# An output projection in seven half-size products instead of eight, on pairs of 128-row blocks

## The chip, the cores and the metric

The kernel runs on one core of a Trainium2 chip. The metric is the device time of one execution in microseconds, here the median of three runs. Five engines work side by side: TensorE (PE in the profile, with its weight loads as PEld), VectorE (DVE), ScalarE (ACT), GpSimd (POOL) and SyncE (SP), which issues nearly all the DMAs here. TensorE writes its sums to PSUM, in banks of 512 columns of f32; VectorE and ScalarE read them from there, GpSimd works on SBUF alone.

## The reference

One token sequence x of 2048 rows and 512 columns goes two ways, and a gate per row mixes the results:

```
a   = x @ dft_hid_re.T ;  b = x @ dft_hid_im.T
A   = dft_seq_re @ a - dft_seq_im @ b                 # 2048 x 2048 by 2048 x 512, twice
q, k, v = split(x @ wqkv), 32 heads of 16
o   = softmax(q k^T / 4, causal, window 256) @ v
B   = o @ wo                                          # 2048 x 512 by 512 x 512
g   = sigmoid(sum(x * gate_w))
out = g * A + (1 - g) * B
```

All is f32. To keep the precision, every f32 operand of a matrix product is split in two parts, hi and lo, and three products are summed: hi hi, hi lo and lo hi (`TERMS`).

## The kernel before

The rows are handled in 16 blocks of 128 (`tb`). Attention runs as a pipeline over four head groups and 32 key blocks; the dense work (projections, then the DFT along the sequence) is a Python generator, `dense`, from which a few TensorE instructions at a time are put between those of attention. TensorE's order is therefore written out by hand. For VectorE, ScalarE, GpSimd and SP a planner sets the order after the first instructions, by its own estimate of when each instruction can start; `behind` and `late` only hold an instruction back until a named earlier one has been issued.

A DFT block (`c_block`, and `c_final` for block 15) takes 16 chunks of 3 matmuls of 512 columns (L528). Its weights come from raw pieces of `cr` and `ci`, 512 KB each, that are loaded ahead into two `raw` buffers and split by VectorE (`split_soon`; the profile shows these under L587, the line of `late`) into three `hi`/`lo` buffers. Finished blocks are scaled by the gate and stored to scratch in DRAM (`r_scr`), and `add_r` lists their numbers in `wait`. The attention output lies in DRAM as well (`o_scr`, transposed, four groups g of 128 rows).

When attention has ended, `attention_done` reuses its large buffers: `fin` in the place of `ring0` holds the split `wo`, `os` in the place of `ring1` holds split attention blocks. From then on `c_part` calls `tail_step` after every fourth chunk, so every twelve DFT matmuls. These calls are the steps, counted from 0 by `clock`. The output projection is done there:

- `wo_prep(tb)` loads one attention block (256 KB, in runs of 512 bytes) and splits it: ScalarE makes hi, VectorE lo (L80, L85). Up to seven blocks are kept ahead.
- `wo_block` runs, three steps later at the earliest and two blocks to a step, 4 groups x 3 terms = 12 matmuls of 512 columns (L811) into one PSUM bank, loads the stored DFT row `r` and adds the two with the gate on VectorE (L813); `tail_step` stores the sum to `out`.

For blocks 14 and 15 the projection comes before the end of the DFT; the sum is kept in `mixed`, and `add_r` and `c_final` add the DFT part to it. `wo` is loaded in `attention_done` into the two `raw` buffers. The steps that begin the two last DFT pieces are in `c_final`: four chunks each at steps 9, 10 and 11, two at step 12, and at the end the last two chunks in halves of 256 columns (L558), each followed by a VectorE instruction (L560) and a store (L561).

PSUM has four banks for `st` (the `ps_a` pool: attention scores, then the projection), two for attention outputs and two for the dense work.

Of the kernel before, what the change touches and what calls it, by code (L numbers as in the profile page):

```python
# [7 lines left out]
F32 = mybir.dt.float32  # L8
F32R = mybir.dt.float32r
AF = mybir.ActivationFunctionType  # L10
OP = mybir.AluOpType
# [3 lines left out]
P = 128  # L15
# [3 lines left out]
NG = 4  # L19
NP = 4  # L20
BQ = 64
NB = S // BQ
WIN = 320
# [4 lines left out]
SWITCH = 6  # L28
# [4 lines left out]
def fnet_window_mix(ctx: ExitStack, tc: tile.TileContext, xT, x, wqk, wv, wr, wi, cr, ci, wo, gw, out):  # L33
    nc = tc.nc

    const = ctx.enter_context(tc.tile_pool(name="const", bufs=1))
    big = ctx.enter_context(tc.tile_pool(name="big", bufs=16))
    st = ctx.enter_context(tc.tile_pool(name="st", bufs=3))
    ev = ctx.enter_context(tc.tile_pool(name="ev", bufs=5))
    at = ctx.enter_context(tc.tile_pool(name="at", bufs=2))  # L40
    ps_a = ctx.enter_context(tc.tile_pool(name="ps_a", bufs=4, space=PSUM))
# [36 lines left out]
    def split(hi, lo, raw, act=False):  # L78
        if act:
            nc.scalar.copy(hi, raw)  # L80
# [4 lines left out]
        return nc.vector.tensor_sub(lo, raw, f(hi))  # L85
# [57 lines left out]
    def pt_raw():  # L143
        return at.tile([P, NP, WIN], F32, name="pt", bufs=4).rearrange("p a b -> p (a b)")[:, :1024]
# [290 lines left out]
    def t_pair(n, p):  # L435
        q0 = n % NB * BQ
        w = min(WIN, S - q0)
        if p == 0:
            if "proj" in have:
                more.append(n)  # L440
            c = (n - more[0]) % 6 * NP * WIN if more else 3072
            if c + NP * WIN <= 3072:
                PT[n] = f(home[:, c:c + NP * WIN].rearrange("p (a b) -> p a b", a=NP))
            else:
                PT[n] = at.tile([P, NP, WIN], F32, name="pt", bufs=4)
        pt = PT[n]
        ps = ps_a.tile([P, 512], F32, name="t", tag="st")
        nc.tensor.matmul(ps[:, :w], PAD[1, n][:, p], ring[0][:, p, q0:q0 + w], start=True, stop=True)  # L448
        nc.scalar.activation(pt[:, p, :w], ps[:, :w], AF.Exp, scale=-1.0)  # L449
        if p % 2:  # L450
            ph = slice(p - 1, p + 1)
            a = pt[:, ph, 0:64]
            nc.gpsimd.affine_select(a, a, pattern=[[0, 2], [2, 64]], compare_op=OP.is_ge, fill=0.0,  # L453
                                    base=1, channel_multiplier=-1)
# [88 lines left out]
    def c_final(get, ab):  # L543
        ps = ps_d.tile([P, 512], F32, name="dc", tag="d")
        g = g1[:, 15:16]
        for j in range(2):
            w = get((1, 30 + j))
            yield from c_part(w, range(16)[8 * j:8 * j + 8 - 2 * j], ab, ps, (0, 13))
            yield
        while wait:  # L550
            tail_step()
        r = mixed.pop(15)
        late(nc.vector.scalar_tensor_tensor, r, ps, g, r, OP.mult, OP.add)
        for c, dma in ((slice(0, 256), nc.sync), (slice(256, 512), nc.scalar)):
            ps2 = ps_a.tile([P, 512], F32, name="t", tag="st")
            for i in (14, 15):
                for a, b in TERMS:
                    nc.tensor.matmul(ps2[:, c], w[a][:, i % 8 * 128:i % 8 * 128 + 128], ab[SC[i]][:, b, c],  # L558
                                     start=i == 14 and a + b == 0, stop=i == 15 and a == 1)
            nc.vector.scalar_tensor_tensor(r[:, c], ps2[:, c], g, r[:, c], op0=OP.mult, op1=OP.add)  # L560
            dma.dma_start(out[15][:, c], r[:, c])  # L561
        yield
# [197 lines left out]
    now = []  # L760
    wait = []
    mixed = {}
    born = {}
    clock = iter(range(99))

    def tail_step():
        t = next(clock)
        for tb in [tb for tb in O if born[tb] < t - 2][:2]:
            if tb in wait:
                wait.remove(tb)  # L770
                ld(out[tb], wo_block(tb, 1))
            else:
                mixed[tb] = wo_block(tb, 0)
        for tb in (*wait[:5], 15, 14, *wait[5:]):
            if tb not in O and tb not in mixed and len(O) < 7 and (tb > now[-1] or tb in wait):
                wo_prep(tb)
                born[tb] = t

    def attention_done():
        fin = const.tile([P, 8192], F32R, name="fin", tag="ring0")  # L780
        ORAW.extend(f(fin[:, 4112 + 512 * i:4624 + 512 * i]).rearrange("p (g t) -> p g t", g=NG) for i in range(7))
        fin = fin[:, 16:4112].rearrange("p (j c h e) -> p j c h e", j=2, c=2, h=2)
        OS.append(const.tile([P, 8, 2, NG, P], F32R, name="os", tag="ring1"))
        for j in range(2):
            raw = st.tile([P, 1024], F32, name="raw", bufs=2)
            ld(raw, wo[j])
            for c in range(2):
                split(fin[:, j, c, 0], fin[:, j, c, 1], raw[:, c * 512:c * 512 + 512])
        FIN.append(fin)

    OS = []
    ORAW = []
    O = {}
    slot = iter(range(99))

    def wo_prep(tb):
        oraw = ORAW[0]
        ORAW.append(ORAW.pop(0))
        ld(oraw, o_scr[tb // 4][:, :, tb % 4 * P:tb % 4 * P + P].rearrange("g p t -> p g t"))
        O[tb] = OS[0][:, next(slot) % 8]  # L800
        split(O[tb][:, 0], O[tb][:, 1], oraw[:], True)

    def wo_block(tb, half):
        o = O.pop(tb)
        r = ev.tile([P, 512], F32, name="ev")
        ld(r, r_scr[half if half or tb < 16 - SWITCH else 2][tb])
        ps = ps_a.tile([P, 512], F32, name="t", tag="st")
        n = 0
        for g in range(NG):
            for a, b in TERMS:  # L810
                nc.tensor.matmul(ps, o[:, a, g], FIN[0][:, g // 2, g % 2, b], start=n == 0, stop=n == 11)  # L811
                n += 1
        nc.vector.scalar_tensor_tensor(r, ps, g0[:, tb:tb + 1], r, op0=OP.mult, op1=OP.add)  # L813
        return r


    stream = dense()
# [46 lines left out]
    for n in range(N + LAG + 1):  # L864
        k = n - LAG
        if k == 0:
            masks.append(n)
        ring_ahead(n + 1)
        if k in (-1, 4):
            v_spread(0 if k < 0 else 4)  # L870
        if k in (-4, -1, 4):
            v_next({-4: 0, -1: 4, 4: 8}[k])
        if n == 0:
            make_pad(0, 0)
        for p in range(NP):
            if n < N:
                s_pair(n, p)
            fill(n)
            visit = p == 0 and (k - summed >= (6 if more else 4) or k == N)
            if 0 <= k < N and not visit:  # L880
                t_pair(k, p)
            if p == 0:
                make_pad(0, n + 1)
                if k >= -1:
                    make_pad(1, k + 1)
            fill(n)
            if visit:
                for j in range(summed, k):
                    pv(j)
                summed = k  # L890
                if k < N:
                    t_pair(k, p)
            for at_n, at_p, do in TURN if n > 12 else FIRST:
                u, j = divmod(n - at_n, 8)
                if p == at_p and j == 0 and 0 <= u < 16:
                    do(u)
            if p == 3 and k % 8 == 6 and 0 <= k < N:
                l_load(k // 8)
            if p == 0 and full:
# [55 lines left out]
```

## Time and profile before

| | |
|---|---|
| median of 3 runs | 850.38 us (850.13 to 850.64) |
| the profiled execution | 850.96 us, its span 849.0 us |
| granted TensorE clock | 1.000 |
| projection matmuls, L811 | 192, 45.5 us busy, mean 392 ns |
| DFT matmuls, L528 | 1530, 344.5 us (hi) and 200.3 us (lo) busy |
| ScalarE cast of an attention block, L80 | 16, mean 621 ns |
| VectorE subtraction of an attention block, L85 | 16, mean 682 ns |
| VectorE gate and sum of a projected block, L813 | 16, mean 748 ns |
| `fin<-o_scr`, `ev<-r_scr` and `out<-ev` loads and stores | 256 KB each |

The busy time of a matmul overlaps that of the next, since they are pipelined: the time from one start to the next is shorter than the mean. Line numbers are those of the kernel before; a helper's line (L56 for loads and stores, L80, L82 and L85 for splits, L587 for what goes through `late`) stands for all its callers, so the names of the tiles tell which work it is. In a line of the timeline the first number is the start, the second the time from the first start to the last end, and x the number of instructions in it.

### The profile page before, as it was taken

Reading aid. Unit: us, or ns where it says so; the run is one execution under the profiler, and the core shown is the slowest. Engines: PE = TensorE matmul, PEld = TensorE weight load, DVE = VectorE, ACT = ScalarE, POOL = GpSimd, SP = SyncE. Lnnn points to the kernel's source line nnn. Section 1 sums busy time; section 2 is a strip of 40 time slices with the busy share of each in tenths; the row PEclk is TensorE's granted clock in tenths of the full one; section 3 lists DMA queues with packets and bytes.
Section 4 is the critical chain, followed back from the end, with each engine's and each line's share of the span. In section 5 each row is a group of like instructions: output and inputs, shape, how many; then the busy total and the mean of one; then the engine's idle time right before and its main releaser. Section 6 shows DMA issues by size and latency. Waiting matters only on the chain.

```text
span 849.0 us, 16711 instructions
## 1 busy us (share of the span) xinstructions
PE 843.7 (99%) x5166; PEld 691.4 (81%) x5166; DVE 611.3 (72%) x1999; ACT 593.6 (70%) x1798; POOL 256.8 (30%) x578
## 2 busy tenths in 40 slices
PE   9999999999999999999999999999999999999998
PEld 6888888888888788888888887888887878878887
DVE  5588978667978787787787886887987864437531
ACT  6488888878888897787877886877777865532100
POOL 8102332233332233342323333343233364620000
PEclk9999999999999999999999999999999999999999
DMA  8776678476765275533454557969774435339732
GB/s 296 244 228 186 214 243 257 181 233 225 216 222 178 63 211 134 171 115 123 137 158 127 177 150 227 308 216 306 254 215 134 138 121 164 128 118 333 225 134 75
DMA packets 94345, 160.99 MB, mean 190 GB/s; under 512 B 26800, under 2 KB 35760, under 8 KB 94256
## 3 DMA queue, kind: packets, MB, share of 16 engines
q1 hardware_dynamic: 93824, 159.28, 60.2%
q8 instruction: 40, 0.66, 0.3%
q10 hardware_dynamic: 432, 0.66, 0.2%
q14 instruction: 49, 0.40, 0.1%
HBM read 108.27 MB, written 51.64 MB: 188 GB/s over the span
## 4 chain that ended last, share of the span: by engine, by line
PE 94%; DMA 2%; DVE 2%; issue 1%; SPq 0%; ACT 0%; DVEq 0%; ACTq 0%
PE dc L528 39%; PE dqk L280 9%; PE dab L303 9%; PE t L448 9%; PE s L366 8%; PE o L474 8%; PE t L811 5%; PE dv L303 5%; DMA raw<-wo 1%; DMA ev<-l_scr 1%; PE s L268 1%; DVE sm L368 1%; PE dv L592 0%; SPq L56 0%; DVE pad L349 0%
## 5 line engine op out<-in xcount | busy, mean ns | idle before, releaser
L528 PE MATMUL dc<-big,hi 128*128 128x512 f32 x1020 | 344.5, 393 | 0.0
L371 ACT ACTIVATE sm<-sm,ml 128x320 f32<-128x320 f32 (+4 forms) x512 | 277.4, 543 | 59.6 <-DVE ml L368 54.1
L368 DVE CUSTOM_DVE_ANT_0 sm<-s,mask 128x320 f32<-128x320 f32 (+4 forms) x512 | 235.0, 464 | 108.6 <-PE s L366 73.2
L449 ACT ACTIVATE pt<-t 128x320 f32<-128x320 f32 (+4 forms) x392 | 159.8, 411 | 87.7 <-PE t L448 82.1
L528 PE MATMUL dc<-big,lo 128*128 128x512 f32 x510 | 200.3, 393 | 0.0
L528 PEld LDWEIGHTS dc<-big,hi 128*128 128x128 f32 x1020 | 180.4, 188 | 22.6
L448 PE MATMUL t<-ring,pad 128*128 128x320 f32 (+4 forms) x512 | 156.8, 306 | 0.1
L453 POOL TENSOR_SCALAR_AFFINE_SELECT pt<-pt 128x128 f32<-128x128 f32 x196 | 71.2, 363 | 283.3 <-ACT pt L449 279.7
L366 PE MATMUL s<-ring,pad 128*128 128x320 f32 (+4 forms) x512 | 155.3, 303 | 0.3 <-DVE ml L368 0.2
L349 DVE TENSOR_SCALAR pad<-ring,half 96x256 fp32r<-96x256 f32 x384 | 120.4, 360 | 11.9 <-PE t L448 11.7
L448 PEld LDWEIGHTS t<-ring,pad 128*128 128x128 f32 x512 | 96.1, 188 | 31.1 <-issue 8.7
L366 PEld LDWEIGHTS s<-ring,pad 128*128 128x128 f32 x512 | 96.2, 188 | 21.7 <-DVE ml L368 2.0
L528 PEld LDWEIGHTS dc<-big,lo 128*128 128x128 f32 x510 | 95.9, 188 | 11.9
L371 ACT ACTIVATION_READ_ACCUMULATOR sm<-sm,ml 128x1 f32 x512 | 97.4, 190 | 0.0
L587 DVE TENSOR_TENSOR lo<-raw,hi 128x512 fp32r<-128x512 f32 x137 | 93.8, 694 | 0.1
L303 PE MATMUL dab<-hi,big 128*128 128x512 f32 x256 | 89.0, 394 | 0.0
L280 PE MATMUL dqk<-big,hi 128*128 128x512 f32 x240 | 85.0, 393 | 0.0
L431 POOL TENSOR_SCALAR vpad<-vr,half 128x256 f32<-128x256 f32 x64 | 61.3, 969 | 65.3 <-PE o L474 30.3
L587 DVE CAST hi<-raw 128x512 fp32r<-128x512 f32 x137 | 57.7, 431 | 20.5 <-PE dc L528 17.0
L347 ACT ACTIVATE pad<-ring,half 96x256 fp32r<-96x256 f32 x128 | 66.8, 522 | 0.0
L457 POOL TENSOR_SCALAR_AFFINE_SELECT pt<-pt 128x128 f32<-128x128 f32 x172 | 60.8, 354 | 0.0
L474 PE MATMUL o<-pt,vpad 128*32 128x320 f32 (+4 forms) x1072 | 57.7, 351 | 0.0
(96 smaller groups left out, 912.5 us busy)
## 6 DMA issues: line engine op xcount, KB each, us to landing
qk_scr<-home SPq DMA_DIRECT2D x32, 512.0 KB
ring<-qk_scr SPq DMA_DIRECT2D x32, 512.0 KB
raw<-cr SPq DMA_DIRECT2D x32, 512.0 KB
raw<-ci SPq DMA_DIRECT2D x32, 512.0 KB
r_scr<-ev SPq DMA_DIRECT2D x42, 256.0 KB
ev<-r_scr SPq DMA_DIRECT2D x42, 256.0 KB
ab_scr<-home SPq DMA_DIRECT2D x20, 512.0 KB
big<-ab_scr SPq DMA_DIRECT2D x20, 512.0 KB
```

Source lines behind the costliest of these rows:

```text
L280: nc.tensor.matmul(ps, w[a][:, c:c + 128], XT[dk, ss][:, b], start=n == 0, stop=n == 11)
L303: nc.tensor.matmul(ps, XT[dk, ss][:, a, c * 128:(c + 1) * 128], wh[b], start=n == 0, stop=n == 11)
L349: nc.vector.tensor_scalar(dst, src, half[:96, h:h + 1], None, op0=OP.mult)
L366: nc.tensor.matmul(ps[:, :w], PAD[0, n][:, p], ring[1][:, p, k0:k0 + w], start=True, stop=True)
L368: mark("dve", nc.vector.tensor_tensor_reduce(out=sm[:, :w], in0=ps[:, :w], in1=mask[:, WIN - w:], scale=1.0, scalar=3e38, op0=OP.add, op1= ...
L371: mark("act", nc.scalar.activation(sm[:, :w], sm[:, :w], AF.Exp, bias=nm[:, c], scale=-1.0, accum_out=l[:, c]))
L448: nc.tensor.matmul(ps[:, :w], PAD[1, n][:, p], ring[0][:, p, q0:q0 + w], start=True, stop=True)
L449: nc.scalar.activation(pt[:, p, :w], ps[:, :w], AF.Exp, scale=-1.0)
L453: nc.gpsimd.affine_select(a, a, pattern=[[0, 2], [2, 64]], compare_op=OP.is_ge, fill=0.0, base=1, channel_multiplier=-1)
L474: nc.tensor.matmul(OT[g, sb][32 * p:32 * p + 32, q - sb * 512:e - sb * 512], v2[:, p], pt[:, p, q - q0:e - q0], start=first, stop=kb == 8 ...
L528: nc.tensor.matmul(ps, w[a][:, i % 8 * 128:i % 8 * 128 + 128], ab[SC[i]][:, b], start=i == ends[0] and a + b == 0, stop=i == ends[1] and a ...
L587: return fn(*args)
```

## The change

The output projection takes the blocks in eight pairs and computes each pair as a 2 x 2 block product: rows (two blocks a and b) by halves of the depth, times halves of the depth by halves of the columns of `wo`. The Strassen-Winograd scheme does this with seven products of half depth and half width (two depth chunks x three terms = 6 matmuls of 256 columns each) in place of eight, with sums of the inputs ahead of it and of the products behind it.

- `wo_fetch` loads `wo` with the last step of the attention loop, into two buffers of the pool of the probability tiles (`pt`), not into `raw`.
- `attention_done` forms four differences of quarters of `wo` (t1 to t4, GpSimd, 512 wide) and splits seven operands in place of four (three casts of them on ScalarE). Six buffers of attention (`vpad`, `pad`) take the raw attention blocks, three pairs of them; t1 to t4 are in four of the same. `rt`, in the place of `home`, holds the r rows of three pairs.
- `wo_load` loads the two attention blocks of a pair, at steps 0, 1 and 4 to 9.
- `wo_split`, two steps later or more (steps 4 to 11), loads the two r rows, makes the four sums s1 to s4 of 128 x 256 on GpSimd, and splits 512, 256 and 1024 columns (ScalarE hi, VectorE lo) into one of two slots of `os`.
- `wo_begin`, at the next step (5 to 12): four products p1, p6, p7, p5, each in a PSUM bank; ScalarE copies p1, VectorE adds p6 to it, and five VectorE operations (`into`) put p7, p5 and that sum (three times) into the rows.
- `wo_end`, at the step after (6 to 13): the closing three products go on top of p1, p7 and p5, and three `into` finish the rows, which are stored or kept in `mixed`.

So within a step TensorE does the three closing products of one pair, the four first ones of the next, and twelve DFT matmuls. `c_final` runs steps until nothing is open, and step 13 (the closing products of the last pair) lies ahead of the last halves.

```diff
-        while wait:
+        while wait or O:
             tail_step()
...
     def tail_step():
         t = next(clock)
-        for tb in [tb for tb in O if born[tb] < t - 2][:2]:
...
+        for stage, at_t in ((wo_end, 6), (wo_split, 4), (wo_begin, 5)):
+            if 0 <= t - at_t < 8:
+                stage(t - at_t)
+        if t < 2 or 4 <= t < 10:
+            wo_load(t if t < 2 else t - 2)
+
+    def wo_fetch():
+        for j in range(2):
+            WO.append(pt_raw())
+            ld(WO[j], wo[j])
 
     def attention_done():
         fin = const.tile([P, 8192], F32R, name="fin", tag="ring0")
...
-        for j in range(2):
-            raw = st.tile([P, 1024], F32, name="raw", bufs=2)
-            ld(raw, wo[j])
-            for c in range(2):
-                split(fin[:, j, c, 0], fin[:, j, c, 1], raw[:, c * 512:c * 512 + 512])
+        fin = fin[:, 16:7184].rearrange("p (m h c e) -> p m h c e", m=7, h=2, c=2)
+        OS.append(const.tile([P, 2, 4096], F32R, name="os", tag="ring1"))
+        RT.append(const.tile([P, 6, 512], F32, name="rt", tag="home"))
+        b11, b12, b21, b22 = (w.rearrange("p (c n e) -> p n c e", c=2, n=2)[:, n] for w in WO for n in range(2))
+        t1, t2, t3, t4 = (const.tile([P, 2, 256], F32, name="tw", tag=f"pad{i}_{j}")[:] for i in range(2)
+                          for j in range(2))
+        for t, x, y in ((t1, b12, b11), (t3, b22, b12), (t2, b22, t1), (t4, b21, t2)):
+            nc.gpsimd.tensor_sub(t, x, y)
+        for m, t in enumerate((b11, b21, b22, t4, t1, t2, t3)):
+            split(fin[:, m, 0], fin[:, m, 1], t, m % 2)
+        for tag in ("vpad0", "vpad1", "pad0_0", "pad0_1", "pad1_0", "pad1_1"):
+            ORAW.append(const.tile([P, NG, P], F32, name="oraw", tag=tag))
         FIN.append(fin)
...
+    def wo_load(i):
+        pair = [15, 14] if i == 2 else [wait.pop(0) for _ in range(2)]
+        raw = []
+        for tb in pair:
+            raw.append(ORAW.pop(0))
+            ORAW.append(raw[-1])
+            ld(raw[-1], o_scr[tb // 4][:, :, tb % 4 * P:tb % 4 * P + P].rearrange("g p t -> p g t"))
+        O[i] = pair, [t[:].rearrange("p g t -> p (g t)") for t in raw]
+
+    def wo_split(i):
+        pair, (a, b) = O[i]
+        k = 4 if i == 2 else i % 2 * 2
+        r = RT[0][:, k], RT[0][:, k + 1]
+        for tb, t in zip(pair, r):
+            with behind("sp"):
+                ld(t, r_scr[2 if i == 2 else 1][tb])
+        extra = at.tile([P, NP, WIN], F32, name="pt", bufs=4).rearrange("p a b -> p (a b)")
+        s1, s2, s3, s4 = (extra[:, 256 * k:256 * k + 256] for k in range(4))
+        nc.gpsimd.tensor_add(s1, b[:, :256], b[:, 256:])
+        nc.gpsimd.tensor_sub(s3, a[:, :256], b[:, :256])
+        nc.gpsimd.tensor_sub(s2, s1, a[:, :256])
+        nc.gpsimd.tensor_sub(s4, a[:, 256:], s2)
+        o = OS[0][:, i % 2, 16:3600].rearrange("p (h m) -> p h m", h=2)
+        for c, src in ((slice(0, 512), a), (slice(512, 768), b[:, 256:]), (slice(768, 1792), extra[:, :1024])):
+            split(o[:, 0, c], o[:, 1, c], src, True)
+        O[i] = pair, r, extra, o.rearrange("p h (m c t) -> p h m c t", m=7, c=2)
+
+    def wo_begin(i):
+        pair, (r1, r2), extra, o = O[i]
...
+        p1, p6, p7, p5 = (ps_a.tile([P, 512], F32, name="t", tag="st")[:, lo] for _ in range(4))
+
+        def product(ps, m, n, start=True):
+            for c in range(2):
+                for a, b in TERMS:
+                    nc.tensor.matmul(ps, o[:, a, m, c], FIN[0][:, n, b, c], start=start and c == 0 and a + b == 0,
+                                     stop=c == 1 and a == 1, skip_group_check=True)
+
+        def into(r, t, g):
+            nc.vector.scalar_tensor_tensor(r, t, g, r, op0=OP.mult, op1=OP.add)
+
+        u, u2 = extra[:, 1024:1280], extra[:, :256]
+        product(p1, 0, 0)
+        nc.scalar.copy(u, p1)
+        product(p6, 4, 5)
+        nc.vector.tensor_add(u2, p6, u)
+        product(p7, 5, 6)
+        into(r2[:, hi], p7, gb)
+        product(p5, 3, 4)
+        into(r2[:, hi], p5, gb)
+        into(r1[:, hi], u2, ga)
+        for c in (lo, hi):
+            into(r2[:, c], u2, gb)
+
+        def rest():
+            product(p1, 1, 1, False)
+            into(r1[:, lo], p1, ga)
+            product(p7, 2, 3, False)
+            into(r2[:, lo], p7, gb)
+            product(p5, 6, 2, False)
+            into(r1[:, hi], p5, ga)
...
+            if k == N - 1 and p == 3:
+                wo_fetch()
```

More of the change, by code (lines that the diff above doesn't have):

```diff
@@ L762, in fnet_window_mix @@
     mixed = {}
-    born = {}
     clock = iter(range(99))
@@ L767, in tail_step @@
         t = next(clock)
-        for tb in [tb for tb in O if born[tb] < t - 2][:2]:
[L769 to L777, printed above, removed]
+        for stage, at_t in ((wo_end, 6), (wo_split, 4), (wo_begin, 5)):
+            if 0 <= t - at_t < 8:
+                stage(t - at_t)
@@ L779, in attention_done @@
+        if t < 2 or 4 <= t < 10:
+            wo_load(t if t < 2 else t - 2)
+    WO = []
+    def wo_fetch():
+        for j in range(2):
+            WO.append(pt_raw())
+            ld(WO[j], wo[j])
     def attention_done():
         fin = const.tile([P, 8192], F32R, name="fin", tag="ring0")
-        ORAW.extend(f(fin[:, 4112 + 512 * i:4624 + 512 * i]).rearrange("p (g t) -> p g t", g=NG) for i in range(7))
-        fin = fin[:, 16:4112].rearrange("p (j c h e) -> p j c h e", j=2, c=2, h=2)
-        OS.append(const.tile([P, 8, 2, NG, P], F32R, name="os", tag="ring1"))
@@ L789, in attention_done @@
         FIN.append(fin)
     OS = []
+    RT = []
     ORAW = []
     O = {}
[L794 to L814, printed above, removed]
+    def wo_load(i):
[6 more added lines that the diff above has]
+        O[i] = pair, [t[:].rearrange("p g t -> p (g t)") for t in raw]
@@ new lines, in wo_begin @@
+    def wo_begin(i):
+        pair, (r1, r2), extra, o = O[i]
+        ga, gb = (g0[:, tb:tb + 1] for tb in pair)
+        lo, hi = slice(0, 256), slice(256, 512)
+        p1, p6, p7, p5 = (ps_a.tile([P, 512], F32, name="t", tag="st")[:, lo] for _ in range(4))
[25 more added lines that the diff above has]
+            into(r1[:, hi], p5, ga)
+            for tb, r in zip(pair, (r1, r2)):
+                if i == 2:
+                    mixed[tb] = r
+                else:
+                    ld(out[tb], r)
+        O[i] = rest
@@ L817, in fnet_window_mix, with wo_end @@
+    def wo_end(i):
+        O.pop(i)()
     stream = dense()
```

## The prediction

> **What bounds the kernel now.** I read the page's engine shares and slices first, to see who is busy at the end.
>
> ```profile
> span 849.0 us, 16711 instructions
> PE 843.7 (99%) x5166; PEld 691.4 (81%) x5166; DVE 611.3 (72%) x1999; ACT 593.6 (70%) x1798; POOL 256.8 (30%) x578
> ...
> PE   9999999999999999999999999999999999999998
> ...
> DVE  5588978667978787787787886887987864437531
> ...
> POOL 8102332233332233342323333343233364620000
> ```
>
> TensorE is busy to the last slice; VectorE and GpSimd thin out in the last four, which hold the output projection. The chain of work that ended last shows whether TensorE sets the end there.
>
> ```profile
> 759.31 6.52 DMA raw<-wo
> ...
> 768.52 5.94 DMA raw<-wo
> ...
> 775.90 4.17 PE t L811 x17
> 780.08 2.74 PE dc L528 x12
> 782.82 5.50 PE t L811 x24
> 788.31 2.72 PE dc L528 x12
> ...
> 832.10 5.50 PE t L811 x24
> 837.59 6.80 PE dc L528 x30
> 844.39 1.44 PE t L558 x12
> 845.83 0.02 issue
> 845.86 0.48 DVE ev L560
> ```
>
> From 775.90 on the chain is one unbroken run of matmuls. A step takes 5.50 us for two output blocks and 2.72 us for twelve DFT matmuls, eight times; then come the last DFT chunks and one VectorE instruction. The windows of two early steps and a late one show the cover.
>
> ```profile
> 765.80:774.00 8.20, 8.20 (x37) 6.78 (x37) 7.51 (x14) 3.10 (x5) 0.00 (x0) 1.00 1.06 322
> 774.00:782.20 8.20, 8.08 (x35) 6.31 (x34) 6.60 (x13) 2.81 (x5) 0.00 (x0) 1.00 1.14 331
> 798.70:806.90 8.20, 8.20 (x38) 6.75 (x37) 2.70 (x4) 1.24 (x2) 0.00 (x0) 1.00 0.34 115
> ```
>
> The columns are TensorE, weight loads, VectorE, ScalarE, GpSimd, then clock, DMA share, GB/s. VectorE is nearly full (7.51 of 8.20) and the DMA engines are full just where the projection starts; later both have room. GpSimd does nothing. So shorter matmul work here is paid out one for one, if the early part doesn't break.
>
> **1. The matmuls.** Per pair of blocks, 2 x 12 matmuls of 512 columns (L811) become 7 products x 2 chunks x 3 terms = 42 of 256 columns. The old spacing, then the only 256-column stream of this kind, at the end:
>
> ```profile
> 774.01 6.06 PE L811 MATMUL t<-fin,os 128*128 128x512 f32 x24
> ...
> 782.65 5.66 PE L811 MATMUL t<-fin,os 128*128 128x512 f32 x24
> ```
>
> ```profile
> 844.46 0.28 PE L558 MATMUL t<-big,lo 128*128 128x256 f32 x1
> ...
> 845.54 0.28 PE L558 MATMUL t<-big,lo 128*128 128x256 f32 x1
> ```
>
> The old pair takes 5.50 us (chain), 229 ns each. The two L558 rows are the third and the twelfth of a run in which every matmul loads its own weights: 1.08 us over nine intervals, 120 ns. So 42 x 0.120 = 5.04 us, 0.46 less per pair, and 8 x 0.46 = **3.7 us less**. The Trainium skill ("TensorE: Matmul & The Clock Gate", Back-to-back issue gap) has N/2.4 + 2.5 ns, so 216 and 109 ns, and by that estimate the saving would be 0.6 us a pair, 4.8 in all. The rows here are 11 to 13 ns above it at either width, and an overhead per matmul hurts the 42 more than the 24.
>
> **2. The start.** The first old run lasts 6.06 us against 5.66: it waited 0.40 us for the split weights. That wait goes; what is late next is the new preparation. The first new pair starts two steps later in the step count than the old (step 5, not 3), so at 774.01 + 2 x 2.73 = 779.5, and its second product, which needs the sums, 0.72 later: 780.2.
>
> wo now lands in the buffers of the last probability tiles, which these matmuls release:
>
> ```profile
> 761.59 0.54 PE L474 MATMUL o<-pt,vpad 128*32 128x128 f32 x16
> ```
>
> So its load leaves at about 761.9 on SP's queue, where the old one left at 759.31; loads queued behind it wait too, the raw DFT pieces among them. With the old 6.5 us it lands at 768.4, and at 765 if the DMA engines are freer (fewer attention blocks are fetched ahead). Then GpSimd makes four 512-wide differences, and for the first pair four 256-wide sums. Its rows, and VectorE's beside them:
>
> ```profile
> L587 POOL TENSOR_TENSOR lo<-raw,hi x5: 1295/1302/1430, 68.0 to 88.2; 128x512 fp32r<-128x512 f32 x5
> ```
>
> ```profile
> 67.95 1.66 DVE L349 TENSOR_SCALAR pad<-ring,half 96x256 fp32r<-96x256 f32 x2
> ```
>
> ```profile
> 68.03 2.72 POOL L587 TENSOR_TENSOR lo<-raw,hi 128x512 fp32r<-128x512 f32 x2
> ```
>
> ```profile
> L349 DVE TENSOR_SCALAR pad<-ring,half x384: 334/345/1392, 31.8 to 750.9; 96x256 fp32r<-96x256 f32 x192
> ```
>
> ```profile
> 757.63 0.78 POOL L453 TENSOR_SCALAR_AFFINE_SELECT pt<-pt 128x128 f32<-128x128 f32 x1 [1.25 <-ACT pt L449]
> ...
> 760.76 0.29 POOL L453 TENSOR_SCALAR_AFFINE_SELECT pt<-pt 128x128 f32<-128x128 f32 x1 [1.25 <-ACT pt L449]
> ```
>
> ```profile
> 757.58 1.37 DVE L587 TENSOR_TENSOR lo<-raw,hi 128x512 fp32r<-128x512 f32 x2
> ...
> 769.62 3.09 DVE L85 TENSOR_TENSOR os<-fin,os 128x512 fp32r<-128x512 f32 x5
> ```
>
> A 512-wide GpSimd two-input operation takes 1.30 us. No row has a 256-wide one: it lies between half (0.65) and the whole (1.30); I take 0.7, near the half, as the work follows the width. Together 4 x 1.30 + 4 x 0.7 = 8.0 us. Then the two engines block each other: a GpSimd select takes 0.78 us beside VectorE's two-input subtraction and 0.29 alone, and L349's median of 0.345 grows to as much as 1.39: its two at 67.95 run into GpSimd's subtractions of 68.03. A GpSimd operation may wait for one VectorE subtraction (0.6 to 0.68): 0 to 8 x 0.68 = 5.4 us in all. After it come ScalarE's cast and VectorE's subtraction of the 1024-wide sums:
>
> ```profile
> 10.81 1.14 ACT L80 CAST hi<-raw 128x512 fp32r<-128x512 f32 x2 [0.34 <-DMA raw<-wv]
> ```
>
> 1.14 us by two 512 casts, and 1.28 for two subtractions (0.60 + 0.68). GpSimd must thus be done by 780.2 - 2.4 = 777.8. Earliest: 765 + 8.0 = 773, early by 5 us. Latest: 768.4 + 8.0 + 5.4 = 781.8, late by 4.0. The middle (766.7 + 8.0 + 2.7 = 777.4) just holds. I book 0.7 us, from 0 to 4.0, and -0.40 for the old wait. Seven weight splits in place of four add three subtractions and no VectorE cast (three of seven casts are ScalarE's): 1.8 us more in a stretch where VectorE has little room; that is within the 4.0.
>
> **3. The steady steps.** A step is 5.04 + 2.72 = 7.76 us of matmuls. VectorE's rows:
>
> ```profile
> 7.97 0.42 DVE L163 TENSOR_TENSOR lo<-pt,hi 128x256 fp32r<-128x256 f32 x1
> 8.30 0.68 DVE L85 TENSOR_TENSOR big<-pt,big 128x512 fp32r<-128x512 f32 x1
> ```
>
> ```profile
> 844.43 0.75 DVE L587 SCALAR_TENSOR_TENSOR ev<-dc,g,ev 128x512 f32<-128x512 f32 x1 [6.05 <-PE dc L528]
> 845.28 1.06 DVE L560 SCALAR_TENSOR_TENSOR ev<-t,g,ev 128x256 f32<-128x256 f32 x2
> ```
>
> Subtractions follow each other every 0.33 us at 256 columns, 0.60 at 512 (3.09 for five), about 1.14 at 1024: 2.07. Six operations that read PSUM (the sum u2 and five `into`), 256 wide, between 0.33 and 0.48: 0.40, so 2.4. Three `into` from u2 in SBUF: 1.0. Own sum **5.5 us of 7.76**, plus 0.2 for the DFT blocks and about 1.0 where pieces are still split. The old step had 2 x (0.60 + 0.75) = 2.7. GpSimd's four sums (2.8 us) can run a step or more ahead, as their blocks are loaded two steps early; ScalarE's casts and one copy (about 2.5) fit easily. I cost this at nothing: PSUM banks come back in time, because the next pair's first product needs the bank freed after the first of three closing products, 1.44 us earlier, and the VectorE operation takes 0.4. If VectorE comes 1.0 us late there, that cover is gone.
>
> On SP's queue, each pair's two r loads wait until the stores of two pairs before have left the same rows of `rt`; they are wanted a step later, so 7.76 less a store is spare; the last store here takes 2.7 us from its data, 845.86 + 0.48, to the span's end. Loads behind them wait as long, and those are for later steps. Hidden.
>
> **4. The end.** The last pair closes after step 12's DFT matmuls, right before the final halves. VectorE gets one more 0.4 us operation ahead of the 0.75 of 844.43; it would delay the first half's by 0 to 0.5, the last not much. The pair's two stores of 256 KB run 2 us ahead of the last two of 128 KB, and at the windows' 322 GB/s each takes 0.8, so 0 to 0.7 of delay. I book 0.3, from 0 to 1.2.
>
> **Sum.** -3.7 - 0.4 + 0.7 + 0.3 = -3.1 us. The profiled execution, 850.96 (span 849.0 and 1.96 around it), gives 847.9; the median of the runs shown is 0.58 lower, so **847.3 us**, 0.36% less. About 0.2%, 1.7 us, is what a measurement of this kernel can tell from no change.
>
> **Rivals.** (a) *The preparation is late.* GpSimd's chain of eight operations, held up by VectorE and by a late wo, stops TensorE at the first pair's second product by 2 to 4 us. For it: VectorE and the DMA engines full there (the first window). Against: two more steps of time, 5.5 us, and fewer loads ahead. Time: 850.4 - 3.7 - 0.4 + 0.3 + (2 to 4) = 848.6 to 850.6.
>
> (b) *VectorE becomes the bound, slower than before.* If each GpSimd sum stops VectorE for its whole length, a step costs VectorE 5.5 + 0.2 + 2.8 = 8.5 us, 9.5 with a piece's split, against 7.76. It decides from 2.1 us of blocking a step on (1.1 with a piece). Six such steps, four with pieces: 4 x 1.7 + 2 x 0.7 = 8.2 us, so 850.4 - 3.1 + 8.2 = about 855. For it: L349's 1.39. Against: a sum can run at any time in the two steps before it is wanted, and VectorE is idle for a quarter of a step. The Trainium skill ("SBUF — State Buffer", SBUF: two separate sides) calls the shared port pair an exclusive lock, "the other fully blocks", taken by a VectorE operation with two SBUF inputs or in a two-port mode; by that rule, the L349 and L453 rows agree, and the PSUM operations are free of it.
>
> (c) *Half width isn't half the time.* If the 42 matmuls, each with its own weights and seven waits, take over 131 ns (5.50 / 42), the change loses by itself; and at 150 ns, the time from a 320-column matmul to the next,
>
> ```profile
> 739.99 0.31 PE L448 MATMUL t<-ring,pad 128*128 128x320 f32 x1
> 740.14 0.62 PE L528 MATMUL dc<-big,hi 128*128 128x512 f32 x2
> ```
>
> it would be 8 x 0.8 = 6.4 us slower, less the old wait and with start and end 857. The 120 ns of L558 speak against it.
>
> **How the numbers follow.** Forecast 0.52 (846.3 to 848.6: the start at 0 to 2, the end at 0 to 1.2); (a) 0.25; (b) 0.18; (c) 0.05. The range runs from 846.2, nothing lost at start and end, to 851.6, the start at 4.0 and the end at 1.2, and leaves out (b), (c) and little else. Faster takes the forecast and a third of (a), 0.60; within 0.2% the rest of (a) and a mild (b), 0.18; slower 0.22.
>
> **What would show it.** Right: 336 projection matmuls at 120 ns, pairs of 5.04 us, no idle of TensorE beyond 1 us in all after 779.5, VectorE some 6 to 7 us in each step's window. The start's step is wrong if weight loads wait for VectorE or ScalarE tiles of the first pair near 780; (b) if they wait for `into` in every step and VectorE's window is full; (c) if the spacing is above 131 ns with no wait. The prediction fails most easily if the planner orders GpSimd's or SP's work otherwise than I assume.

## The result and the profile after

The changed kernel takes 857.93 us (median of six runs, 856.48 to 859.79), the kernel before 850.25 on the same chips (849.29 to 851.48): a ratio of 1.0093 [1.0077, 1.0108]. It is slower by 0.9%, where 0.36% less was forecast. The profiled execution takes 858.08 us, its span is 856.1, 7.1 longer than before. The page of the changed kernel, shares and slices:

```profile
span 856.1 us, 17153 instructions
...
PE 842.6 (98%) x5310; PEld 697.4 (81%) x5310; DVE 651.6 (76%) x2066; ACT 604.9 (71%) x1817; POOL 293.7 (34%) x614
...
PE   9999999999999999999999999999999999997898
...
DVE  5588977667978787687787787797888765449986
...
POOL 8102332233331323342323333343232364545520
```

TensorE's work shrank a little (843.7 to 842.6) and the span grew, so TensorE now waits: its slices show a 7 and an 8 near the end. There VectorE reads 9, 9, 8 where it read 7, 5, 3, and GpSimd 5, 5, 2 where it had nothing. The chain of work that ended last in the changed kernel (start, length, engine and work):

```profile
776.92 5.54 DMA oraw<-o_scr
...
782.60 0.74 POOL pt L819
783.33 0.89 POOL pt L820
...
784.24 5.05 DMA oraw<-o_scr
789.28 1.78 DVE hi L587 x2
...
791.65 2.36 DVE lo L587 x2
794.01 0.33 DVE pt L847
794.34 0.40 DVE rt L841
...
794.79 5.90 PE t L837 x36
...
811.80 5.03 PE t L837 x42
816.84 2.75 PE dc L528 x12
...
849.34 2.15 PE t L837 x18
851.50 1.45 PE t L558 x12
852.95 0.03 issue
852.97 0.48 DVE rt L560
```

Before, TensorE alone carried the chain from 775.90 on. Now it holds unbroken only after 807. Up to 794.79 the chain runs through a late load of attention blocks, GpSimd's sums, and above all VectorE: the splits of DFT pieces (`hi`, `lo`, L587), and only then `u2` (L847) and the `into` (L841) for which TensorE has been waiting. From 811.80 the steps are the ones forecast, 5.03 us for 42 projection matmuls and 2.75 for twelve DFT matmuls.

What TensorE waited for in the projection (us in total, times, longest), and its timeline at the longest wait; VectorE's and GpSimd's timelines show what led to it (start, length, work, in brackets the idle time before):

```profile
PE t L837 <- DVE rt L841: 6.6, 2, 6.4
PE t L837 <- DVE os L85: 1.1, 1, 1.1
PE t L837 <- ACT pt L845: 0.3, 1, 0.3
```

```profile
794.79 5.90 PE L837 MATMUL t<-fin,os 128*128 128x256 f32 x36 [6.43 <-DVE rt L841]
```

```profile
765.98 2.98 DVE L587 CAST hi<-raw 128x512 fp32r<-128x512 f32 x2
768.88 1.52 DVE L82 CAST fin<-tw 128x512 fp32r<-128x512 f32 x1
...
785.30 2.37 DVE L587 TENSOR_TENSOR lo<-raw,hi 128x512 fp32r<-128x512 f32 x2
...
793.93 0.41 DVE L847 TENSOR_TENSOR pt<-t,pt 128x256 f32<-128x256 f32 x1
```

```profile
763.97 3.26 POOL L789 TENSOR_TENSOR tw<-pt 128x512 f32<-128x512 f32 x2 [2.49 <-DMA pt<-wo]
767.18 2.93 POOL L789 TENSOR_TENSOR tw<-pt,tw 128x512 f32<-128x512 f32 x2
...
773.11 1.06 POOL L822 TENSOR_TENSOR pt<-oraw,pt 128x256 f32<-128x256 f32 x1
```

While GpSimd makes the four differences of `wo`, two casts of VectorE take 2.98 us; the first row of experiment 1's fence below has two in 0.76 without GpSimd. TensorE's closing products of the first pair go on top of p7, so they need the `into` (L841) that reads p7 first. On VectorE this `into` stands behind `u2` (L847); `u2` needs the first two products, over by 784, and starts at 793.93. The windows of the changed kernel (TensorE, weight loads, VectorE, ScalarE, GpSimd, clock, DMA share, GB/s):

```profile
765.80:774.00 8.20, 8.20 (x38) 6.76 (x37) 8.20 (x8) 2.02 (x4) 8.04 (x7) 1.00 0.40 137
...
782.20:790.00 7.80, 5.81 (x34) 4.77 (x34) 7.54 (x8) 2.34 (x4) 7.33 (x8) 1.00 1.12 352
790.00:798.00 8.00, 3.21 (x15) 3.22 (x16) 7.96 (x14) 0.82 (x2) 6.02 (x7) 0.57 0.16 61
...
814.00:822.00 8.00, 8.00 (x58) 7.51 (x57) 7.36 (x15) 2.57 (x5) 4.15 (x6) 1.00 0.51 154
```

In the first window VectorE is busy all through and finishes only 8 instructions, against 14 in 7.51 us before. The third window has TensorE at 3.21 of 8.00 and a granted clock of 0.57.

The balance: adding up, in the spacing of matmuls from the first product on, everything above the normal step, TensorE waits 9.38 us (before: 0.51) and loses another 1.24 at half clock. This is more than the three waits above, as it counts from one start of a matmul to the next. So -3.8 (8 x (5.50 - 5.03)) - 0.5 + 9.4 + 1.2 = 6.3 of the 7.1 us. Of the rest, 0.4 lies ahead of the first product, at 779.89 instead of 779.5, and about 0.2 is the twelve DFT matmuls of a step, 2.75 us and 2.72 before; the last 0.2 stays open.

### The profile page after: what moved, and what is told of

It is laid out like the page before. It is cut to its first block, busy times and chain, and to the rows that moved or that the text cites. A ratio compares the mean times of both kernels' runs of the same rounds, so it can differ in the third digit from the quotient of the medians.

```text
span 856.1 us, 17153 instructions
## 1 busy us (share of the span) xinstructions
PE 842.6 (98%) x5310; PEld 697.4 (81%) x5310; DVE 651.6 (76%) x2066; ACT 604.9 (71%) x1817; POOL 293.7 (34%) x614
## 4 chain that ended last, share of the span: by engine, by line
PE 94%; DVE 3%; DMA 1%; issue 1%; POOL 0%; ACT 0%; DVEq 0%; SPq 0%; POOLq 0%; ACTq 0%
PE dc L528 39%; PE dab L303 10%; PE dqk L280 9%; PE t L448 9%; PE s L366 8%; PE o L474 8%; PE dv L303 5%; PE t L837 4%; DMA oraw<-o_scr 1%; PE s L268 1%; DVE lo L587 1%; DVE fin L85 0%; DVE hi L587 0%; PE dv L592 0%; DVE fin L82 0%
## 5 line engine op out<-in xcount | busy, mean ns | idle before, releaser
L587 DVE TENSOR_TENSOR lo<-raw,hi 128x512 fp32r<-128x512 f32 x137 | 97.0, 716 | 0.1
L587 DVE CAST hi<-raw 128x512 fp32r<-128x512 f32 x137 | 62.6, 466 | 19.1 <-PE dc L528 15.1
L453 POOL TENSOR_SCALAR_AFFINE_SELECT home<-home 128x128 f32<-128x128 f32 x60 | 26.6, 443 | 96.3 <-ACT home L449 95.5
```

The costliest lines, as they stand in the source:

```text
L587: return fn(*args)
```

## The experiments

The theories, as the expectations call them by letter or in words: GpSimd's sums and VectorE's operations exclude each other, and VectorE loses its time through that (L); GpSimd's chain of sums is late by itself (C); the planner's order on VectorE puts other splits ahead of what TensorE waits for (O); late loads on SP's queue together with such an order (Q); VectorE's own work is too much (W); the preparation as a burst onto a full VectorE (B). All experiments are edits of the changed kernel; they ran on three chips, and each ratio is to the kernel before on the same chip; where an edit adds or removes lines, the numbers of the lines below it shift (L841 is L832 in experiment 1 and L851 in 9 and 11).

**1. No sums.** The splits read the raw quarters and blocks in place of GpSimd's eight results, so the output is another; splits and matmuls stay, but for the one split of 1024 columns, made as two of 512.

```diff
-        for t, x, y in ((t1, b12, b11), (t3, b22, b12), (t2, b22, t1), (t4, b21, t2)):
-            nc.gpsimd.tensor_sub(t, x, y)
-        for m, t in enumerate((b11, b21, b22, t4, t1, t2, t3)):
+        for m, t in enumerate((b11, b21, b22, b21, b12, b22, b12)):
...
-        nc.gpsimd.tensor_add(s1, b[:, :256], b[:, 256:])
...
-        for c, src in ((slice(0, 512), a), (slice(512, 768), b[:, 256:]), (slice(768, 1792), extra[:, :1024])):
+        for c, src in ((slice(0, 512), a), (slice(512, 768), b[:, 256:]), (slice(768, 1280), a), (slice(1280, 1792), b)):
```

> Left out: GpSimd's eight kinds of sums. The weight operands that were differences are split from plain quarters of wo, and the sums of the blocks from the raw blocks, so the output is another; TensorE's, ScalarE's and VectorE's instructions stay the same but for one 1024-wide split made as two of 512. Theory L (lock): in the changed kernel VectorE lost about 11 us between 764 and 806 because GpSimd's two-input sums and VectorE's operations on SBUF exclude each other; without the sums TensorE's waits in the projection fall from 9.4 us to under 1.5 and the time is 846 to 849 us. Rival Q (queues and order): the late loads behind a raw piece on SP's queue and a piece's split put ahead of the pair's sums on VectorE cost the time; the waits stay above 4 us, 853 us or more. Rival W: VectorE's own work is too much; the waits stay above 4 us.

Measured: 848.01 us, ratio to before 0.9958 [0.9941, 0.9975]; waits 0.93 us, clock 1.0 throughout. About ten microseconds hang on the sums, and without them the prediction's arithmetic for TensorE holds. (Q) and (W) alone, which expected waits above 4 us to stay, fall. This run doesn't say whether it is the waiting for the sums' results or their presence.

**5. Idle sums.** As experiment 1, but GpSimd still makes all sums, into places that no split reads; the output is again another. (The number is that of the run.)

```diff
-        for m, t in enumerate((b11, b21, b22, t4, t1, t2, t3)):
+        for m, t in enumerate((b11, b21, b22, b21, b12, b22, b12)):
...
-        for c, src in ((slice(0, 512), a), (slice(512, 768), b[:, 256:]), (slice(768, 1792), extra[:, :1024])):
+        for c, src in ((slice(0, 512), a), (slice(512, 768), b[:, 256:]), (slice(768, 1280), a), (slice(1280, 1792), b)):
```

> As the run without sums (848.0 us), but GpSimd does its sums all the same, into places that no split reads: the engines meet at SBUF as in the changed kernel, while no split waits for a sum. Left out: the sums as operands, so the output is another. Theory L (the two engines stop each other): VectorE is held up as in the changed kernel, TensorE waits 5 us or more and the time is 853 us or more. Rival C (the chain load, sum, cast, subtraction is too long, and the holding up matters little): as without sums, 847 to 849.5 us.

Measured: 861.98 us, 1.0134 [1.0107, 1.016]: 14 us more than experiment 1, although no split needs a sum. The same VectorE work in experiment 1, then in experiment 5, then GpSimd's in experiment 5 (timelines):

```profile
767.09 0.76 DVE L587 CAST hi<-raw 128x512 fp32r<-128x512 f32 x2
...
768.10 2.50 DVE L85 TENSOR_TENSOR fin<-pt,fin 128x512 fp32r<-128x512 f32 x4
```

```profile
771.65 1.83 DVE L587 CAST hi<-raw 128x512 fp32r<-128x512 f32 x2
...
774.28 4.08 DVE L85 TENSOR_TENSOR fin<-pt,fin 128x512 fp32r<-128x512 f32 x4
```

```profile
775.52 1.17 POOL L820 TENSOR_TENSOR pt<-oraw 128x256 f32<-128x256 f32 x1
776.65 1.17 POOL L822 TENSOR_TENSOR pt<-oraw,pt 128x256 f32<-128x256 f32 x1
777.78 1.17 POOL L821 TENSOR_TENSOR pt<-pt,oraw 128x256 f32<-128x256 f32 x1
```

Four subtractions take 2.50 us alone and 4.08 beside GpSimd, from one start to the next 1.13 us, the rhythm of GpSimd's sums, which take 0.74 alone (782.60 in the chain above): the engines take turns. (C) falls as the sole cause: with nobody waiting for the sums, the time doesn't come back. What stays mixed in the 14 us is the planner's order, which differs between the two kernels: here TensorE's longest wait, 3.8 us at 779.55, is of the DFT for the subtraction of a piece. Of the 13.0 us between the two profiled spans (858.4 and 845.4), 1.8 are there already at the last matmul of attention (763.01 and 761.24), so they can't come from the sums.

The group rows from 763 us on put a size on it: casts and subtractions of the DFT pieces and one PSUM operation (count, busy, mean ns) in experiment 1, then in the changed kernel:

```profile
L587 DVE CAST hi<-raw 128x512 fp32r<-128x512 f32 x10 | 3.8, 424 | 4.0 <-DMA raw<-ci 3.6 <-PE dc L528 0.3
L587 DVE TENSOR_TENSOR lo<-raw,hi 128x512 fp32r<-128x512 f32 x10 | 6.4, 688 | 0.0
L832 DVE SCALAR_TENSOR_TENSOR rt<-t,g,rt 128x256 f32<-128x256 f32 x40 | 19.2, 480 | 8.6 <-PE t L828 7.8 <-DMA rt<-r_scr 0.7
```

```profile
L587 DVE CAST hi<-raw 128x512 fp32r<-128x512 f32 x10 | 8.2, 853 | 0.4 <-PE dc L528 0.4
L587 DVE TENSOR_TENSOR lo<-raw,hi 128x512 fp32r<-128x512 f32 x10 | 9.7, 1004 | 0.0
L841 DVE SCALAR_TENSOR_TENSOR rt<-t,g,rt 128x256 f32<-128x256 f32 x40 | 19.1, 476 | 6.6 <-PE t L837 6.5
```

The pieces alone cost VectorE 4.4 + 3.3 = 7.7 us more. In experiment 5, whose splits read what experiment 1's read, the seven subtractions of `wo` from its raw quarters take 1302 ns each, and 690 in experiment 1. The operation with one input in PSUM costs the same in the changed kernel as without the sums. The Trainium skill ("SBUF — State Buffer", Who interferes with whom) says that a VectorE instruction with at most one SBUF input, outside its two-port modes, doesn't contend with GpSimd; the 480 and 476 ns agree. It calls the port pair that the two share an exclusive lock; the turns of 1.13 us agree roughly, as they are a little less than the two operations one after the other (0.60 + 0.74 = 1.34 us).

**2 and 3. Fewer SBUF operations on one side.** Experiment 2 gives GpSimd's sums to VectorE (`nc.gpsimd.tensor_sub` and `tensor_add` become `nc.vector`), experiment 3 the casts of the DFT pieces to ScalarE:

```diff
-            jobs.append(lambda c=c: late((nc.vector if masks else nc.gpsimd).tensor_copy, hi[:, c], raw[:, c]))
+            jobs.append(lambda c=c: late(nc.scalar.copy if WO else (nc.vector if masks else nc.gpsimd).tensor_copy,
+                                         hi[:, c], raw[:, c]))
```

> All sums on VectorE in place of GpSimd, nothing else. L: VectorE is rid of about 11 us of standing still and gets 4 x 0.6 us for the weights and 4 x 0.33 us per pair, about 6 us in the same stretch; TensorE waits 3 to 6 us and the time is 851 to 855 us, less than with GpSimd. W: more work on a full engine, so more than 858 us. Q: about the same, 857 to 859 us.

> From the load of wo on, the casts (hi) of the raw DFT pieces go to ScalarE, which idles there; their subtractions stay on VectorE. That takes some ten two-port casts of 0.4 us, which also meet the sums of GpSimd, off VectorE. L and W: 4 to 6 us less on VectorE, 851 to 855 us. Q: less than 1.5 us of change.

Measured: 856.14 us, 1.0063 [1.0043, 1.0083], and 855.82, 1.0053 [1.0032, 1.0074]. Both win 2 to 3 us on the changed kernel and fall just outside the range of every theory: less than (L) expected, more than (Q) did in experiment 3, and (W)'s more than 858 didn't come in experiment 2. In experiment 2 nothing is blocked any more, but VectorE has the sums in its own queue, and the planner puts pieces and sums of later pairs ahead of the first pair's last sum (781.12) and of the split of its sums (785.66): TensorE waits 3.1 us for the cast of these sums and 3.9 for the subtraction, 9.13 us in all. Experiment 3 has 6.97 us of waits and half clock from 787.4 to 797.6. There the exclusion seems to fall on GpSimd. Its first sum for the second pair, and the split of that pair's sums on VectorE (timelines):

```profile
778.47 3.89 POOL L820 TENSOR_TENSOR pt<-oraw 128x256 f32<-128x256 f32 x1 [4.88 <-DMA oraw<-o_scr]
```

```profile
785.67 1.35 DVE L85 TENSOR_TENSOR os<-pt,os 128x1024 fp32r<-128x1024 f32 x1 [3.92 <-ACT os L80]
```

A sum of 0.74 us is recorded as 3.89: VectorE works without a gap from 777.80 to 781.75, and the sum ends 0.6 us after that, at 782.36. VectorE itself then stands idle for 3.92 us behind a split that needs the sums. Taking away a part of the load doesn't clear the queue.

**4. One step later.** Every stage but the loads one step later; the first product is at 782.58 and not 779.89, so the first pair's preparation has 2.7 us more.

```diff
-        for stage, at_t in ((wo_end, 6), (wo_split, 4), (wo_begin, 5)):
+        for stage, at_t in ((wo_end, 7), (wo_split, 5), (wo_begin, 6)):
...
-        pair = [15, 14] if i == 2 else [wait.pop(0) for _ in range(2)]
+        pair = [15, 14] if i == 1 else [wait.pop(0) for _ in range(2)]
```

> Each pair is split, begun and ended one step (2.7 us of DFT matmuls) later, with the pair of blocks 15 and 14 second and not third, loads at the same steps; the last pair then closes with no DFT matmuls ahead of it. If the preparation is only late by a fixed time, the waits of 9.4 us shrink by 2.7 us and the slow clock goes with them: 853 to 855.5 us. If VectorE is behind in every early step (L and W as a rate, not as a delay), less than 1.5 us is won.

Measured: 859.53 us, 1.0104 [1.0084, 1.0124]; waits 10.3 us, 7.94 of them at 788.79. The step more won nothing; it isn't a fixed delay that a later start would cover. VectorE first stands idle for 3.92 us, until 787.38, as in experiment 3 (GpSimd's first sum for the second pair is recorded as 4.03 us here). Then its time goes to splits which the planner puts there: from 788.66 on it works off six operations on DFT pieces, and `u2` comes at 795.07.

**6, 7 and 8. VectorE in program order.** From the end of attention on VectorE takes its instructions in the order of the program, not the planner's: alone (6), with experiment 3's casts (7), with experiment 2's sums (8).

```diff
+        ctx.enter_context(tc.manual_schedule(engines={mybir.EngineType.PE, mybir.EngineType.DVE}))
         fin = const.tile([P, 8192], F32R, name="fin", tag="ring0")
```

> The changed kernel with VectorE's instructions from the end of attention on in the order of the program text, not in the planner's. Theory O (order): the pair's own sums (the first ones of the chain that frees the PSUM banks) stood behind pieces' splits and later pairs' work; in program order TensorE's longest wait falls from 6.6 us to under 2 and the time to 849 to 853 us. L alone: VectorE is still held up by 11 us in the same stretch and waits in another place; 856 us or more.

> The same, and the casts of the raw DFT pieces on ScalarE as in the run before (855.8 us with the planner's order). O and L together: each takes its own part, 847 to 851 us. If only one of them counts, no better than the better of the two alone.

> VectorE in program order and all the sums on VectorE (856.1 us with the planner's order, where sums of two later pairs stood ahead of the first pair's). O: that order was the reason for its waits of 9.1 us; now under 3 us, 847 to 851 us. W (too much own work on VectorE): 854 us or more.

Measured: 859.83 us, 1.0107 [1.0092, 1.0122]; 856.72, 1.007 [1.0055, 1.0085]; 859.11, 1.0094 [1.0077, 1.0111]. TensorE's waits in experiment 6, then in 7 (us in total, times, longest):

```profile
PE dc L528 <- DVE lo L587: 9.0, 1, 9.0
PE t L838 <- DVE rt L842: 0.8, 1, 0.8
```

```profile
PE dc L529 <- DVE lo L588: 7.9, 1, 7.9
```

The times expected for (O) didn't come: program order is no remedy. The wait in the projection is nearly gone, and a wait of the same size stands at 768.3 instead: the preparation of all of `wo` lies ahead of the next DFT pieces, and the DFT stops for them. That VectorE has too much to do there is not shown, since it stands still within this very wait (experiment 6, timeline):

```profile
773.07 0.69 DVE L85 TENSOR_TENSOR fin<-tw,fin 128x512 fp32r<-128x512 f32 x1 [2.48 <-ACT fin L80]
```

It waits for a cast of the fourth difference, which GpSimd starts only at 771.13, behind two block sums; 2.14 us more of such idle time end at 766.83, and experiment 7 has the same 2.48. So one order makes the projection late, the other the DFT. In experiment 8 the wait is 4.9 us at the start, and further ones of 0.7 to 1.4 follow in the later steps; its 859.11 us are what (W) expected, so with all sums on VectorE its own work does count.

**9 to 12. The preparation spread out.** VectorE in program order, all casts of weights and pieces on ScalarE, the differences of `wo` on VectorE, and the preparation of `wo` cut into eleven parts, one after every fourth DFT matmul. In 9 and 11 GpSimd makes the block sums, in 10 and 12 VectorE; 11 and 12 have experiment 4's extra step.

```diff
+        if n % 4 == 0 and prep:
+            prep.pop(0)()
...
-        for t, x, y in ((t1, b12, b11), (t3, b22, b12), (t2, b22, t1), (t4, b21, t2)):
-            nc.gpsimd.tensor_sub(t, x, y)
...
+        prep.extend([diff(t1, b12, b11), cut(0, b11), diff(t3, b22, b12), diff(t2, b22, t1), cut(4, t1), cut(5, t2),
+                     cut(6, t3), diff(t4, b21, t2), cut(1, b21), cut(3, t4), cut(2, b22)])
```

> VectorE in program order, all casts of the weights and of the raw pieces on ScalarE, the weights' differences on VectorE, and the weights' preparation spread over steps 0 to 3 (one piece of it every four matmuls) between the pieces' splits; the blocks' sums stay on GpSimd. Theory B (burst): what stops TensorE is 11 us of VectorE held up plus the weights' preparation, all within the five steps before the first product; in program order the later steps ran without waits over 1 us. With the burst spread and relieved, waits fall below 3 us and the time is 847 to 851 us. If the sums on GpSimd still hold VectorE up by 5 us or more, 852 or more.

> The same with the blocks' sums on VectorE too, so that nothing meets GpSimd. B: VectorE's own work in the first five steps is then about 14 us of 14; waits 1 to 4 us there, and up to 1 us in each later step, as in the run with sums on VectorE in program order (5.5 + 1.4 + 0.8 of 7.76 us a step): 848 to 853 us.

> As the first of these, and each pair one step later (the pair of 15 and 14 second). B: the early waits go, as there are 2.7 us more; 846.5 to 849 us. If the holding up by GpSimd is a rate and no burst, no better than without the delay.

> As the second of these, and each pair one step later. B: early waits go, the later steps' waits of up to 1 us stay: 847 to 851 us.

Measured, in that order: 852.33 us, 1.0017 [1.0004, 1.0031]; 853.51, 1.0036 [1.0021, 1.005]; 850.13, 0.9991 [0.9976, 1.0006]; 852.88, 1.0022 [1.001, 1.0035]. All four lie above the times expected for (B), by 0.5 to 1.9 us; experiment 9's falls where 5 us or more of holding up by GpSimd's sums were expected. From experiment 7 to 9 4.4 us go, and no wait of the DFT is left. So relieving and spreading the burst helps, but which part of it does is not shown: the differences and the weights' casts moved to other engines at the same time. Experiment 11 is level with the kernel before. Its profiled execution, with 848.56 us one of its fastest (median 850.13), has 2.19 us of TensorE waits and a clock that never falls in the projection. TensorE's waits in experiment 9 and in 11:

```profile
PE t L847 <- DVE rt L851: 2.9, 2, 2.2
```

```profile
PE t L847 <- DVE rt L851: 0.9, 2, 0.5
```

With the block sums on VectorE it gets worse: a steady window of experiment 12,

```profile
814.00:822.00 8.00, 7.87 (x55) 7.24 (x54) 7.63 (x18) 2.45 (x4) 0.00 (x0) 1.00 0.62 196
```

has VectorE at 7.63 of 8.00 us, and TensorE waits 0.3 to 1.0 us in most of the steps, after 1.9 at 796.49. So with the preparation spread out GpSimd is the better place for the four sums of a pair. For the burst at the start the runs lean the other way: with all sums on VectorE, the wait there is 4.9 us and not 9.0 (experiments 8 and 6), but no run moved the start's sums alone. No version that computes the whole result beats the kernel before.

## Why the prediction was wrong, step by step

**1. The matmuls: right.** Forecast 5.04 us a pair, 3.7 less in all; measured 5.03, 3.8 less. Experiment 1 shows that it is paid out when nothing blocks: 2.8 us less than the kernel before on its chip (848.01 and 850.82), where 3.1 was forecast. Rival (c) is out.

**2. The start: the step that failed.** "I book 0.7 us, from 0 to 4.0" asks when GpSimd's chain is done, and the chain was in time. GpSimd's first difference of `wo` starts at 763.97, ahead of the earliest 765, and the last sum for the first pair (773.11 above) ends at 774.2, ahead of the 777.8 needed. The exclusion of the two engines was charged to GpSimd alone (0 to 5.4 us of waiting), in a window whose own row showed VectorE at 7.51 of 8.20. The same exclusion takes the time from VectorE: 7.7 us on the DFT pieces alone. VectorE had no idle time from 763.9 to 782.6, and whatever came after was late. The split of the first pair's sums starts at 780.85, so the second product waits 1.4 us, which is inside the booked range; behind it pieces, the next pair's splits, `u2` and `into` are late too, and most of TensorE's 9.4 us of waits, about 8, comes there. The booked term was 0.3 net of the old wait; the runs show about 10 (9.4 + 1.2 - 0.5) from this one queue. How these divide between the exclusion and the planner's order stays open.

**3. The steady steps: right from 811.80 on, wrong ahead of it.** "I cost this at nothing" holds for the later steps: VectorE 7.36 of 8.00 us beside 4.15 of GpSimd, and TensorE without a gap. Between 782 and 808 the cover was gone: "If VectorE comes 1.0 us late there, that cover is gone" named the place and missed how late: `u2` started about 10 us after its products, since the splits of pieces for later steps are put ahead of it. The cover was also worked out for another need, the bank for the next pair's first product; TensorE stopped for 6.6 us ahead of the first pair's own closing product on p7, which needs the `into` of the step before. The last sentence on what would fail, the planner's order, was right as a warning; experiments 6 to 8 show that program order in its place doesn't mend it.

"Hidden", of SP's queue, was wrong in one place. SP's timeline of the changed kernel:

```profile
764.96 0.32 SPq L56 DMA_DIRECT2D o_scr<-ev  x1
774.75 0.33 SPq L56 DMA_DIRECT2D raw<-ci  x1
```

Nothing leaves for 9.8 us. The profile puts 9.4 us of that down to a subtraction (`lo`) of a DFT piece on VectorE: the piece load waits for the `raw` buffer that the delayed split frees. The next pair's blocks stand behind it and land at 782.46, where the chain picks them up. So a part of (Q), the late loads, is there as a consequence; no run took it apart from the rest.

**4. The end: forecast 0.3, measured about 0.** The last VectorE instruction starts 3.1 us before the span's end (856.1 - 852.97), and 849.0 - 845.86 = 3.1 before.

**The rivals.** (a) described a late chain on GpSimd, worth 2 to 4 us; for the first pair, of which it spoke, the chain wasn't late. (b) had the mechanism and the sign, and its about 855 was near; but it put the price into each steady step (8.5 us against 7.76), where it was not paid, and missed the start. By its own test, waits for `into` in every step with VectorE's window full, it would have been called wrong. Its weight against it, "VectorE is idle for a quarter of a step", is a mean over a step without a piece; the stretch that mattered had none. A cost in no term at all is the clock: 1.24 us. The range's ends, 846.2 and 851.6, come to 846.3 and 851.5 by the prediction's own terms; nothing hangs on that.

## What to carry to other kernels

Where two engines exclude each other, charge the time to both queues, and first of all to the one that has no room in the window where the new work starts; a preparation that is in time itself can still push everything behind it. A saving on the engine that bounds is worth what the start of the stage leaves of it, so spread its preparation over the steps ahead in parts, with the order written out, and look in that order for an instruction that waits for another engine: everything behind it waits too. To tell a late result from a blocked engine, leave the work in place and read nothing from it.

## What the runs showed of the hardware

GpSimd's two-input f32 operation of 256 columns takes 0.74 us alone and 1.17 beside VectorE's subtractions, VectorE's 512-column subtraction 0.60 alone (3.09 for five) and 1.13 beside them, its cast 0.42 alone (424 ns) and up to 1.5 beside GpSimd's 512-column ones (768.88). Turns aren't always kept: behind a run of VectorE operations without a gap, single GpSimd sums are recorded as 3.89 and 4.03 us (experiments 3 and 4).

The clock, too, follows the waits: the last matmul before the stop starts at 788.07, and the trace has the granted clock at 0.5 from 791.0 to 797.8, 3 us beyond the end of the stop at 794.79. The Trainium skill ("TensorE: Matmul & The Clock Gate", What's actually happening) gives half rate after an idle window of about 3.4 us and full rate after about 3.4 us of work; 2.9 us after the last start and 3.0 after the stop's end agree roughly. But the length of a wait alone doesn't decide: in experiments 1, 9 and 11, where no wait was longer than 2.4 us, the clock never fell in the projection, while in experiment 3 it fell at 787.39, after a wait of 2.0 us that had ended at 787.00. Once at half, it stayed there for 3.41, 6.83 or 10.24 us in these runs (experiments 10, 4 and 3).
